# Attention and a two-layer MLP on one core: the exponentials instead of V as the stationary operand of the second attention product, normalised on the way out of PSUM, with the loads on SyncE's queue

## The chip, the cores and the metric

The kernel runs on one core of a Trainium2 chip. The metric is device time in microseconds (us). Before the change three runs gave a median of 557.68 us (556.79 to 560.31).

## The reference

```python
# q, k, v: [8, 12, 448, 64] float32; w_in: [768, 2048], w_out: [2048, 768]
scores = scale * np.matmul(q, k.transpose(0, 1, 3, 2))
scores = scores - np.max(scores, axis=-1, keepdims=True)
attn = np.exp(scores)
attn = attn / (np.sum(attn, axis=-1, keepdims=True) + 1e-09)
attn_out = np.matmul(attn, v)
x = attn_out.transpose(0, 2, 1, 3).reshape(B * S, H * D)     # 3584 x 768
h = x @ w_in
g = np.maximum(0.01 * h, h)
out = g @ w_out                                              # 3584 x 768
```

## The kernel before

Two heads of one batch element make a *unit*; there are 48 units, six to each of the eight batch elements. A sequence of 448 positions is cut into four chunks of 112 (`SC`, `NSC`), taken with a stride of four so that each partition reads contiguous memory. The work of a unit is:

- `load` fetches q, k and v in float32, three DMAs of 224 KB issued by GpSimd. `cast` turns them into bf16 on GpSimd, v into one of four tiles `v_sb` whose other 64 columns hold ones.
- `transposes` turns q and k on TensorE (eight transposes into the PSUM tile `tr`), and VectorE copies the result out as `qkT`.
- `scores` makes the transposed scores, keys on partitions, for one chunk of keys and both heads; `expo` takes the exponential on ScalarE into `e`. Four such chunks make a unit. The PSUM tiles `sc` have two buffers.
- `pv(u, j)` multiplies for head j: V with its ones is stationary (112 x 128), the exponentials stream past with 448 columns, four matmuls accumulate over the key chunks. The result has head dimension on partitions; 64 of its rows all hold the sum of the exponentials. VectorE copies it out as `t`, and a DMA on SyncE's queue brings one row of sums into a small tile.
- `recips` inverts the sums on VectorE, writes them to DRAM by one DMA, and reads them back by two, spread over 64 partitions each (`rb`). `muls` multiplies `t` by `rb` on VectorE into `xT`, the MLP's input, in two pieces for each head since the MLP's token blocks are cut at multiples of 128.
- `mlp(i)` takes 384 or 512 tokens: 96 matmuls with `w_in` (line 233), leaky ReLU on ScalarE, then 32 matmuls for each 128 tokens with `w_out` (line 245), copied out by VectorE and stored by SyncE's queue.

Every engine runs its instructions in the order in which they are written here. `slots(u)` gives eight steps of work of unit u, in which `pv` belongs to unit u-1 and `recips` and `muls` to unit u-2. The loop at the end writes the steps of six units and hands out the matmuls of one `mlp` evenly between them. The first `mlp` begins after the first step of unit 8, so units 0 to 7 run without MLP work beside them; the last `mlp` stands alone at the end. The weights are loaded by GpSimd's queue, two pieces at a time in the first four units, and each is cast from float32 by its DMA.

Of the kernel before, what the change touches and what calls it, by code (L numbers as in the profile page):

```python
# [9 lines left out]
F32 = mybir.dt.float32  # L10
BF16 = mybir.dt.bfloat16
AX = mybir.ActivationFunctionType
PSUM = bass.MemoryType.PSUM
DRAM = bass.MemoryType.DRAM


@with_exitstack
def kernel(
# [27 lines left out]
    const_pool = ctx.enter_context(tc.tile_pool(name="const", bufs=1))  # L46
    w_pool = ctx.enter_context(tc.tile_pool(name="weights", bufs=1))
    ld_pool = ctx.enter_context(tc.tile_pool(name="ld", bufs=6))
    cast_pool = ctx.enter_context(tc.tile_pool(name="cast", bufs=3))
    v_pool = ctx.enter_context(tc.tile_pool(name="vones", bufs=1))  # L50
    qk_pool = ctx.enter_context(tc.tile_pool(name="qk", bufs=3))
    exp_pool = ctx.enter_context(tc.tile_pool(name="exp", bufs=3))
    t_pool = ctx.enter_context(tc.tile_pool(name="pvt", bufs=3))
    r_pool = ctx.enter_context(tc.tile_pool(name="rec", bufs=3))
    xT_pool = ctx.enter_context(tc.tile_pool(name="xT", bufs=3))
    h_pool = ctx.enter_context(tc.tile_pool(name="h", bufs=2))
    o_pool = ctx.enter_context(tc.tile_pool(name="o", bufs=3))
    d_pool = ctx.enter_context(tc.tile_pool(name="drec", bufs=4, space=DRAM))

    ps_s = ctx.enter_context(tc.tile_pool(name="ps_s", bufs=2, space=PSUM))  # L60
    ps_tr = ctx.enter_context(tc.tile_pool(name="ps_tr", bufs=1, space=PSUM))
    ps_pv = ctx.enter_context(tc.tile_pool(name="ps_pv", bufs=1, space=PSUM))
    ps_mm = ctx.enter_context(tc.tile_pool(name="ps_mm", bufs=2, space=PSUM))

    ident = const_pool.tile([P, P], BF16)
    make_identity(nc, ident)

    NV = 4  # L70
    v_sb = [v_pool.tile([SC, 2, NSC, 2 * D], BF16, name=f"v{i}") for i in range(NV)]
    for t in v_sb:
        nc.vector.memset(t[:, 0, :, D:], 1.0)
        nc.vector.memset(t[:, 1, :, :D], 1.0)

    w_in_sb = w_pool.tile([P, KD, DF], BF16)
    w_out_sb = w_pool.tile([P, MD, DM], BF16)
# [4 lines left out]
    q_sb = {}  # L82
    k_sb = {}

    def load(u):
        if u >= NU:
            return
        b, hp = divmod(u, HP)  # L90
        raw[u] = []
        for a, name in ((q, "fq"), (k, "fk"), (v, "fv")):
            t = ld_pool.tile([SC, 2, NSC, D], F32, name=name)
            nc.gpsimd.dma_start(  # L94
                out=t.rearrange("p h so d -> p h (so d)"),
                in_=a[b, 2 * hp:2 * hp + 2].rearrange("h (p so) d -> p h (so d)", so=NSC),
            )
            raw[u].append(t)

    def cast(u):  # L100
# [5 lines left out]
        nc.gpsimd.tensor_copy(q_sb[u].rearrange("p so h d -> p h so d"), fq)  # L106
        nc.gpsimd.tensor_copy(k_sb[u].rearrange("p so h d -> p h so d"), fk)  # L107
        for j in range(2):
            nc.gpsimd.tensor_copy(v_sb[u % NV][:, j, :, j * D:(j + 1) * D], fv[:, j])  # L109

    load(0)
    cast(0)
    load(1)
    load(2)
    load(3)
    cast(1)
    for i in range(4, 6):
        load(i)
# [6 lines left out]
    def load_w(n):  # L125
        for _ in range(n):
            if w_steps:
                o, i = w_steps.pop(0)
                nc.gpsimd.dma_start(out=o, in_=i)


    qk_t = {}
    e_t = {}
    pv_s = {}
    bc_t = {}
    xT = [None] * (B + 1)

    def get_xT(i):
        if xT[i] is None:
            xT[i] = xT_pool.tile([P, KD, 4 * P], BF16, name="xT")  # L140
        return xT[i]

    def transposes(u):
        b, hp = divmod(u, HP)
        tr = ps_tr.tile([P, 2, S], BF16, name="tr")
        for i, src in enumerate((q_sb[u], k_sb[u])):
            for so in range(NSC):
                nc.tensor.transpose(  # L148
                    tr[:, i, ts(so, SC)], src[:, so], ident[:SC, :SC]
                )  # L150
        qk_t[u] = qk_pool.tile([P, 2, S], BF16, name="qkT")
        nc.vector.tensor_copy(qk_t[u], tr)  # L152

    sc_t = {}
# [10 lines left out]
            )  # L165

    def expo(u, c):
        if u not in e_t:
            e_t[u] = exp_pool.tile([SC, 2, NSC, S], BF16, name="e")
        nc.scalar.activation(e_t[u][:, :, c, :], sc_t.pop((u, c))[:, :, :S], AX.Exp, scale=scale)  # L170

    def pv(u, j):
        b, hp = divmod(u, HP)
        ps = ps_pv.tile([P, S], F32, name="pv")
        for c in range(NSC):
            nc.tensor.matmul(  # L176
                ps, v_sb[u % NV][:, j, c, :], e_t[u][:, j, c, :],
                start=(c == 0), stop=(c == NSC - 1),
            )
        t = t_pool.tile([P, S], F32, name=f"t{j}")  # L180
        nc.vector.tensor_copy(t, ps)  # L181
        pv_s[u, j] = t
        if j == 0:
            bc_t[u] = r_pool.tile([SC, 2, NSC], F32, name="sums")
        row = t[D:D + 1, :] if j == 0 else t[0:1, :]
        nc.sync.dma_start(out=bc_t[u][:, j, :], in_=row)

    def recips(u):
        rec = r_pool.tile([SC, 2, NSC], F32, name="rec")
        nc.vector.reciprocal(rec, bc_t[u])  # L190
        d = d_pool.tile([2, S], F32, name="d")
        nc.sync.dma_start(out=d.rearrange("j (p c) -> p j c", c=NSC), in_=rec)
        rb = r_pool.tile([P, S], F32, name="rb")
        for j in range(2):
            nc.sync.dma_start(out=rb[ts(j, D), :], in_=d[j:j + 1, :].to_broadcast([D, S]))  # L195
        bc_t[u] = rb

    def muls(u):
        b, hp = divmod(u, HP)
        lo, hi = b * S, (b + 1) * S  # L200
        for j in range(2):
            pl = slice(j * D, (j + 1) * D)
            for i in (b, b + 1):
                a, z = max(lo, cuts[i]), min(hi, cuts[i + 1] if i < B else hi)
                if a >= z:
                    continue
                x = get_xT(i)
                nc.vector.tensor_mul(  # L208
                    x[pl, hp, a - cuts[i]:z - cuts[i]],
                    pv_s[u, j][pl, a - lo:z - lo],  # L210
                    bc_t[u][pl, a - lo:z - lo],
                )
        del pv_s[u, 0], pv_s[u, 1], bc_t[u], e_t[u], qk_t[u]


    def store(o, t0):
# [38 lines left out]
    def slots(u):  # L255

        on = u < NU

        def s0():
            if on:  # L260
                scores(u, 0)
                scores(u, 1)
                expo(u, 0)
            load(u + 6)
            if u < 6:
                load_w(2)

        def s1():
            if on:
                expo(u, 1)  # L270
            if u >= 2:
                recips(u - 2)

        def s2():
            if 1 <= u <= NU:
                pv(u - 1, 0)

        def s3():
            cast(u + 2)

        def s4():
            if on:
                scores(u, 2)
                scores(u, 3)
                expo(u, 2)

        def s5():
            if on:
                expo(u, 3)

        def s6():
            if 1 <= u <= NU:
                pv(u - 1, 1)

        def s7():
            if u + 1 < NU:
                transposes(u + 1)
            if u >= 2:
                muls(u - 2)

        return [s0, s1, s2, s3, s4, s5, s6, s7]

# [48 lines left out]
```

## Time and profile before

| | before |
|---|---|
| median of 3 runs | 557.68 us |
| the profiled execution | 556.75 us |
| its span, first to last instruction | 555.0 us |
| TensorE busy in matmuls | 478.5 us (86%) |
| VectorE, ScalarE, GpSimd busy | 215.2, 231.3, 202.1 us |
| mean granted TensorE clock | 0.937 of 2.4 GHz |

The profiled execution took 1.75 us more than its span, and the median of the runs is 0.93 us above it. TensorE's busy time counts the modelled end of each matmul, so matmuls overlap in it; where its pace matters, the distance from one start to the next is the better reading. The busy share is also a mean over a first stage, in which TensorE often stands still, and a long middle in which it seldom does.

### The profile page before, as it was taken

To read this page: it belongs to the slowest core of one execution; us is meant where nothing else is said; L and a number is where in the kernel's file an instruction comes from. 1 tells how busy PE (TensorE), PEld (TensorE's weight loads), DVE (VectorE), ACT (ScalarE), POOL (GpSimd) and SP (SyncE) were. 2 spreads that over 40 slices of the span, in tenths; PEclk is the share of its full clock that TensorE was granted. 3 is DMA by queue.
4 is the path that set the end of the run, shared out by engine and by line. 5 is a ranking of instruction groups with operands and counts; after the bars stand their busy time and mean duration, and the time that the engine had idled before them with its cause. 6 is when DMAs were issued, how large, how long until landed. Compare 5 with 4: busy or idle time off the path is not lost.

```text
span 555.0 us, 7636 instructions
## 1 busy us (share of the span) xinstructions
PE 478.5 (86%) x2816; PEld 237.6 (43%) x2816; DVE 215.2 (39%) x400; ACT 231.3 (42%) x321; POOL 202.1 (36%) x350
## 2 busy tenths in 40 slices
PE   2744447999899999999599999999699999996996
PEld 1211113455444554555244554555244555552453
DVE  2221335444433564444234545464253553341011
ACT  3332223563346334654165335644365246601400
POOL 8963724454532433643225335455141210000000
PEclk9998555999989999999799999999899999997999
DMA  5999944344533354535433436354341222122013
GB/s 147 249 230 242 242 109 103 98 118 120 156 96 83 89 155 123 135 90 154 113 82 94 122 102 172 97 145 115 95 118 30 79 62 50 31 63 60 1 28 87
DMA packets 52774, 62.21 MB, mean 112 GB/s; under 512 B 28672, under 2 KB 39936, under 8 KB 52736
## 3 DMA queue, kind: packets, MB, share of 16 engines
q0 software_dynamic: 16768, 39.33, 27.8%
q1 hardware_dynamic: 35968, 22.38, 16.6%
q8 instruction: 22, 0.36, 0.3%
q14 instruction: 16, 0.13, 0.1%
HBM read 56.62 MB, written 11.18 MB: 122 GB/s over the span
## 4 chain that ended last, share of the span: by engine, by line
PE 65%; DMA 22%; DVE 7%; SPq 2%; issue 2%; POOL 2%; DVEq 0%; POOLq 0%
PE mm L233 25%; PE mm L245 19%; PE pv L176 11%; DMA d<-rec 8%; DMA sums<-t 7%; DMA rb<-d 7%; PE sc L160 6%; DVE xT L208 3%; PE tr L148 3%; DVE qkT L152 2%; SPq L195 1%; DVE o L250 1%; DMA fv<-in_v_dram 1%; SPq L224 1%; POOL fq L94 0%
## 5 line engine op out<-in xcount | busy, mean ns | idle before, releaser
L170 ACT ACTIVATE e<-sc 112x896 bf16<-112x896 f32 x192 | 168.5, 915 | 188.8 <-PE sc L160 188.6
L233 PE MATMUL mm<-xT,w_in_sb 128*128 128x384 bf16 (+1 forms) x768 | 173.0, 364 | 20.9 <-DVE xT L208 19.4
L245 PE MATMUL mm<-w_out_sb,h 128*128 128x384 bf16 x896 | 162.1, 326 | 0.8 <-DVE o L250 0.6
L176 PE MATMUL pv<-e,v 112*128 112x448 bf16 x384 | 100.9, 390 | 29.9 <-DVE t L181 29.9
L109 POOL CAST v<-fv 112x256 bf16<-112x256 f32 x96 | 38.3, 404 | 230.9 <-PE pv L176 230.6
L181 DVE COPY t<-pv 128x448 f32<-128x448 f32 x96 | 59.6, 620 | 149.0 <-PE pv L176 148.7
L233 PEld LDWEIGHTS <-w_in_sb 128*128 128x128 bf16 x768 | 72.0, 100 | 102.7 <-issue 47.7
L238 ACT ACTIVATE h<-mm 128x384 bf16<-128x384 f32 (+1 forms) x128 | 69.9, 546 | 109.2 <-PE mm L233 109.1
L208 DVE TENSOR_TENSOR xT<-t,rb 64x384 bf16<-64x384 f32 (+2 forms) x144 | 87.1, 630 | 68.2 <-DMA rb<-d 67.0
L245 PEld LDWEIGHTS <-h 128*128 128x128 bf16 x896 | 83.6, 98 | 67.0 <-issue 13.7
L176 PEld LDWEIGHTS <-v 112*128 112x128 bf16 x384 | 38.9, 103 | 74.7 <-issue 47.8
L160 PE MATMUL sc<-qkT 64*112 64x448 bf16 x384 | 63.4, 411 | 8.6 <-DVE qkT L152 6.4
L250 DVE COPY o<-mm 128x384 f32<-128x384 f32 x56 | 31.1, 555 | 63.6 <-PE mm L245 63.1
L152 DVE COPY qkT<-tr 128x896 bf16<-128x896 bf16 x48 | 30.0, 624 | 33.5 <-PE tr L148 32.8
L160 PEld LDWEIGHTS <-qkT 64*112 64x112 bf16 x384 | 18.7, 135 | 45.6 <-DVE qkT L152 24.8
L94 POOL DMA_DIRECT2D fv<-in_v_dram x48 | 31.9, 664 | 11.9 <-DMA w_in_sb<-in_moe_w_in_dram 6.5
L106 POOL CAST q<-fq 112x512 bf16<-112x512 f32 x48 | 34.0, 708 | 4.2 <-PE tr L148 1.5
L94 POOL DMA_DIRECT2D fk<-in_k_dram x48 | 31.9, 665 | 7.2 <-DMA w_out_sb<-in_moe_w_out_dram 4.6
L94 POOL DMA_DIRECT2D fq<-in_q_dram x48 | 32.1, 668 | 4.6 <-issue 0.2
L107 POOL CAST k<-fk 112x512 bf16<-112x512 f32 x48 | 31.8, 662 | 0.1
L148 PE MATMUL tr<-ident,q 112*128 112x112 bf16 x192 | 19.3, 228 | 11.2 <-POOL q L106 11.2
L148 PEld LDWEIGHTS <-q 112*128 112x128 bf16 x192 | 15.4, 106 | 21.1 <-POOL q L106 12.4
(14 smaller groups left out, 52.8 us busy)
## 6 DMA issues: line engine op xcount, KB each, us to landing
fq<-in_q_dram POOLq DMA_DIRECT2D x48, 224.0 KB, 3.4
fk<-in_k_dram POOLq DMA_DIRECT2D x48, 224.0 KB, 3.9
fv<-in_v_dram POOLq DMA_DIRECT2D x48, 224.0 KB, 4.2
rb<-d SPq DMA_DIRECT2D x96, 112.0 KB, 3.0
w_in_sb<-in_moe_w_in_dram POOLq DMA_DIRECT2D x4, 768.0 KB, 12.7
w_out_sb<-in_moe_w_out_dram POOLq DMA_DIRECT2D x4, 768.0 KB, 17.7
out_dram<-o SPq DMA_DIRECT2D x8, 336.0 KB, 3.3
out_dram<-o SPq DMA_DIRECT2D x8, 288.0 KB, 2.7
```

The costliest lines, as they stand in the source:

```text
L94: nc.gpsimd.dma_start(out=t.rearrange("p h so d -> p h (so d)"), in_=a[b, 2 * hp:2 * hp + 2].rearrange("h (p so) d -> p h (so d)", so=NSC),)
L109: nc.gpsimd.tensor_copy(v_sb[u % NV][:, j, :, j * D:(j + 1) * D], fv[:, j])
L148: nc.tensor.transpose(tr[:, i, ts(so, SC)], src[:, so], ident[:SC, :SC])
L152: nc.vector.tensor_copy(qk_t[u], tr)
L160: nc.tensor.matmul(ps[:, j, :S], qk_t[u][j * D:(j + 1) * D, 1, ts(c, SC)], qk_t[u][j * D:(j + 1) * D, 0, :], start=True, stop=True,)
L170: nc.scalar.activation(e_t[u][:, :, c, :], sc_t.pop((u, c))[:, :, :S], AX.Exp, scale=scale)
L176: nc.tensor.matmul(ps, v_sb[u % NV][:, j, c, :], e_t[u][:, j, c, :], start=(c == 0), stop=(c == NSC - 1),)
L181: nc.vector.tensor_copy(t, ps)
L208: nc.vector.tensor_mul(x[pl, hp, a - cuts[i]:z - cuts[i]], pv_s[u, j][pl, a - lo:z - lo], bc_t[u][pl, a - lo:z - lo],)
L233: nc.tensor.matmul(ps[:, :n], w_in_sb[:, kk, ts(m, P)], get_xT(i)[:, kk, :n], start=(kk == 0), stop=(kk == KD - 1),)
L238: nc.scalar.activation(h[:, m, :n], ps[:, :n], AX.Prelu, alpha=0.01)
L245: nc.tensor.matmul(ps[:, :NW], h[:, m, ts(c, P)], w_out_sb[:, m, ts(w, NW)], start=(m == 0), stop=(m == MD - 1),)
```

## The change

`pv` swaps its operands. For each chunk of 112 queries the exponentials (112 keys x 128 columns, of which 112 are the queries and 16 run on into the next bytes) are stationary, and V with a single column of ones (65 columns) streams past, accumulated over four chunks of keys: 16 matmuls a head instead of four. The result has queries on partitions and its sum in column 64, so VectorE takes the reciprocal of four values for each partition from PSUM and multiplies straight out of PSUM into a bf16 tile `x`. `x_transposes` then turns `x` by four TensorE transposes for each unit, and VectorE copies them into `xT`. The copies `t`, the DMAs of sums, `d` and `rb`, and the products from `t` and `rb` are gone. The loads are issued by SyncE's queue (one of the first by ScalarE's), all casts of v take one instruction, casts run three units ahead instead of two, buffers of `v_sb` and the casts become five and four, the weights are issued one piece at a time (one ahead of the loop, one each in units 0 to 2 and 5 to 8), and each `mlp` begins six steps earlier, right behind the step that holds the last `x_transposes` it needs.

```diff
-    v_sb = [v_pool.tile([SC, 2, NSC, 2 * D], BF16, name=f"v{i}") for i in range(NV)]
+    v_sb = [v_pool.tile([SC, 2, NSC, D + 1], BF16, name=f"v{i}") for i in range(NV)]
+    EL = 2 * NSC * S
+    e_sb = [exp_pool.tile([SC, EL + P - SC], BF16, name=f"e{i}") for i in range(NE)]
...
-    def load(u):
+    def load(u, queues=(nc.sync,) * 3):
...
-            nc.gpsimd.dma_start(
+            eng.dma_start(
...
-        for j in range(2):
-            nc.gpsimd.tensor_copy(v_sb[u % NV][:, j, :, j * D:(j + 1) * D], fv[:, j])
+        by[2](v_sb[u % NV][:, :, :, :D], fv)
...
+    load(0, (nc.sync, nc.scalar, nc.sync))
+    for i in range(1, 6):
+        load(i)
...
+    cast(0, (nc.vector.tensor_copy, nc.scalar.copy, nc.gpsimd.tensor_copy))
+    load_w()
+    cast(1)
+    cast(2)
...
     def pv(u, j):
-        ps = ps_pv.tile([P, S], F32, name="pv")
-        for c in range(NSC):
-            nc.tensor.matmul(
-                ps, v_sb[u % NV][:, j, c, :], e_t[u][:, j, c, :],
-                start=(c == 0), stop=(c == NSC - 1),
-            )
-        t = t_pool.tile([P, S], F32, name=f"t{j}")
-        nc.vector.tensor_copy(t, ps)
...
+        e, vt = e_sb[u % NE], v_sb[u % NV]
+        ps = ps_pv.tile([P, NSC, D + 1], F32, name="pv")
+        for qc in range(NSC):
+            for c in range(NSC):
+                at = (j * NSC + c) * S + qc * SC
+                nc.tensor.matmul(
+                    ps[:, qc, :], e[:, at:at + P], vt[:, j, c, :],
+                    start=(c == 0), stop=(c == NSC - 1),
+                )
         if j == 0:
-            bc_t[u] = r_pool.tile([SC, 2, NSC], F32, name="sums")
-        row = t[D:D + 1, :] if j == 0 else t[0:1, :]
-        nc.sync.dma_start(out=bc_t[u][:, j, :], in_=row)
+            x_t[u] = x_pool.tile([SC, NSC, 2, D], BF16, name="x")
+        rec = r_pool.tile([SC, NSC, 1], F32, name="rec")
+        nc.vector.reciprocal(rec, ps[:SC, :, D:])
+        nc.vector.tensor_mul(
+            x_t[u][:, :, j, :], ps[:SC, :, :D], rec.to_broadcast([SC, NSC, D])
+        )
...
-    def recips(u):
...
-    def muls(u):
+    def x_transposes(u):
         b, hp = divmod(u, HP)
         lo, hi = b * S, (b + 1) * S
+        tr = ps_tr.tile([P, 2, S], BF16, name="tr")
+        for so in range(NSC):
+            nc.tensor.transpose(tr[:, 0, ts(so, SC)], x_t[u][:, so], ident[:SC, :SC])
+        for i in (b, b + 1):
+            a, z = max(lo, cuts[i]), min(hi, cuts[i + 1] if i < B else hi)
+            if a < z:
+                nc.vector.tensor_copy(
+                    get_xT(i)[:, hp, a - cuts[i]:z - cuts[i]], tr[:, 0, a - lo:z - lo]
+                )
...
         def s0():
-            load(u + 6)
-            if u < 6:
-                load_w(2)
         def s1():
-            if u >= 2:
-                recips(u - 2)
+            if 2 <= u <= NU + 1:
+                x_transposes(u - 2)
         def s3():
-            cast(u + 2)
+            load(u + 6)
         def s5():
+            cast(u + 3)
+            if u <= 2 or 5 <= u <= 8:
+                load_w()
         def s7():
-            if u >= 2:
-                muls(u - 2)
...
+    begin = [8 * (HP * (i + 1) + 1) + 2 for i in range(B)]
     transposes(0)
-    for i in range(B + 1):
-        first = 0 if i == 0 else HP * i + 2
-        last = HP * (i + 1) + 2 if i < B else first
-        work = [s for u in range(first, min(last, NU + 2)) for s in slots(u)]
-        atoms = mlp(i - 1) if i > 0 else iter(())
+    for s in steps[:begin[0]]:
+        s()
+    for i in range(B):
+        work = steps[begin[i]:begin[i + 1]] if i + 1 < B else []
+        atoms = mlp(i)
```

## Rows read from the trace of the kernel before

**Rows 1.** Windows by stage: length, busy us (count) by engine, clock, DMA share, GB/s

```profile
0.00:95.60 95.60, 47.10 (x196) 18.22 (x196) 26.04 (x57) 28.96 (x34) 58.50 (x105) 0.77 0.86 189
95.60:500.60 405.00, 386.53 (x2399) 196.98 (x2398) 182.92 (x332) 192.75 (x272) 143.58 (x246) 0.98 0.39 103
500.60:506.40 5.80, 1.23 (x7) 0.47 (x6) 1.28 (x3) 0.00 (x0) 0.00 (x0) 0.94 0.18 40
506.40:555.00 48.60, 43.68 (x219) 21.96 (x218) 4.98 (x9) 9.56 (x16) 0.00 (x0) 0.92 0.15 41
```

**Rows 2.** TensorE's waits, first 95 us: waiter, releaser, total us, times, longest

```profile
PE pv L176 <- DVE t L181: 29.9, 5, 11.2
PE tr L148 <- POOL q L106: 11.2, 3, 5.6
```

**Rows 3.** Timeline of VectorE and TensorE around one stall of the first stage

```profile
55.25 0.69 DVE L208 TENSOR_TENSOR xT<-t,rb 64x384 bf16<-64x384 f32 x2 [10.73 <-DMA rb<-d]
...
59.35 0.53 PE L176 MATMUL pv<-e,v 112*128 112x448 bf16 x1 [11.25 <-DVE t L181]
```

**Rows 4.** TensorE's waits from 95 us to the end

```profile
PE mm L233 <- DVE xT L208: 19.4, 7, 5.8
```

**Rows 5.** TensorE's timeline of the end: start us, length us, instructions

```profile
500.57 1.24 PE L233 MATMUL mm<-xT,w_in_sb 128*128 128x512 bf16 x5
506.38 22.90 PE L233 MATMUL mm<-xT,w_in_sb 128*128 128x512 bf16 x91 [4.57 <-DVE xT L208]
529.12 20.96 PE L245 MATMUL mm<-w_out_sb,h 128*128 128x384 bf16 x128
```

**Rows 6.** TensorE's timeline of one unit in the middle stage

```profile
463.02 0.59 PE L160 MATMUL sc<-qkT 64*112 64x448 bf16 x4
463.54 1.48 PE L233 MATMUL mm<-xT,w_in_sb 128*128 128x384 bf16 x8
464.85 0.92 PE L176 MATMUL pv<-e,v 112*128 112x448 bf16 x4
465.61 1.47 PE L233 MATMUL mm<-xT,w_in_sb 128*128 128x384 bf16 x8
...
470.24 0.36 PE L148 MATMUL tr<-ident,q 112*128 112x112 bf16 x4
470.44 0.36 PE L148 MATMUL tr<-ident,k 112*128 112x112 bf16 x4
...
471.52 0.59 PE L160 MATMUL sc<-qkT 64*112 64x448 bf16 x4
```

**Rows 7.** TensorE's timeline in the first stage: end of unit 0, one unstalled unit

```profile
10.06 0.62 PE L160 MATMUL sc<-qkT 64*112 64x448 bf16 x2 [0.19 <-ACT e L170]
...
25.01 0.99 PE L160 MATMUL sc<-qkT 64*112 64x448 bf16 x4 [0.72 <-DVE qkT L152]
25.93 1.68 PE L176 MATMUL pv<-e,v 112*128 112x448 bf16 x4
27.54 0.99 PE L160 MATMUL sc<-qkT 64*112 64x448 bf16 x4
...
29.93 0.58 PE L148 MATMUL tr<-ident,q 112*128 112x112 bf16 x4
30.31 0.58 PE L148 MATMUL tr<-ident,k 112*128 112x112 bf16 x4
31.61 0.62 PE L160 MATMUL sc<-qkT 64*112 64x448 bf16 x2 [0.72 <-DVE qkT L152]
```

**Rows 8.** Groups by line and shape: busy us, mean ns, idle before

```profile
L170 ACT ACTIVATE e<-sc 112x896 bf16<-112x896 f32 x192 | 168.5, 915 | 188.8 <-PE sc L160 188.6
L208 DVE TENSOR_TENSOR xT<-t,rb 64x384 bf16<-64x384 f32 x48 | 37.0, 770 | 34.9 <-DMA rb<-d 34.2
L190 DVE RECIPROCAL rec<-sums 112x8 f32<-112x8 f32 x48 | 9.7, 203 | 20.3 <-DMA sums<-t 19.2
```

**Rows 9.** Window of the heaviest loading, same columns as the first group

```profile
20.00:48.00 28.00, 17.09 (x71) 6.18 (x68) 6.65 (x14) 9.40 (x12) 19.84 (x34) 1.00 1.20 234
```

More of the change, by code (lines that the diff above doesn't have):

```diff
@@ L13 @@
 PSUM = bass.MemoryType.PSUM
-DRAM = bass.MemoryType.DRAM
 @with_exitstack
@@ L48 @@
     ld_pool = ctx.enter_context(tc.tile_pool(name="ld", bufs=6))
-    cast_pool = ctx.enter_context(tc.tile_pool(name="cast", bufs=3))
+    cast_pool = ctx.enter_context(tc.tile_pool(name="cast", bufs=4))
     v_pool = ctx.enter_context(tc.tile_pool(name="vones", bufs=1))
     qk_pool = ctx.enter_context(tc.tile_pool(name="qk", bufs=3))
-    exp_pool = ctx.enter_context(tc.tile_pool(name="exp", bufs=3))
-    t_pool = ctx.enter_context(tc.tile_pool(name="pvt", bufs=3))
-    r_pool = ctx.enter_context(tc.tile_pool(name="rec", bufs=3))
+    exp_pool = ctx.enter_context(tc.tile_pool(name="exp", bufs=1))
+    r_pool = ctx.enter_context(tc.tile_pool(name="rec", bufs=4))
+    x_pool = ctx.enter_context(tc.tile_pool(name="x", bufs=3))
     xT_pool = ctx.enter_context(tc.tile_pool(name="xT", bufs=3))
@@ L57 @@
     o_pool = ctx.enter_context(tc.tile_pool(name="o", bufs=3))
-    d_pool = ctx.enter_context(tc.tile_pool(name="drec", bufs=4, space=DRAM))
     ps_s = ctx.enter_context(tc.tile_pool(name="ps_s", bufs=2, space=PSUM))
@@ L63 @@
     ps_mm = ctx.enter_context(tc.tile_pool(name="ps_mm", bufs=2, space=PSUM))
-    ident = const_pool.tile([P, P], BF16)
-    make_identity(nc, ident)
-    NV = 4
-    v_sb = [v_pool.tile([SC, 2, NSC, 2 * D], BF16, name=f"v{i}") for i in range(NV)]
-    for t in v_sb:
-        nc.vector.memset(t[:, 0, :, D:], 1.0)
-        nc.vector.memset(t[:, 1, :, :D], 1.0)
+    NV = 5
+    v_sb = [v_pool.tile([SC, 2, NSC, D + 1], BF16, name=f"v{i}") for i in range(NV)]
+    NE = 3
+    EL = 2 * NSC * S
+    e_sb = [exp_pool.tile([SC, EL + P - SC], BF16, name=f"e{i}") for i in range(NE)]
     w_in_sb = w_pool.tile([P, KD, DF], BF16)
@@ L91, in load @@
         raw[u] = []
-        for a, name in ((q, "fq"), (k, "fk"), (v, "fv")):
+        for a, name, eng in zip((q, k, v), ("fq", "fk", "fv"), queues):
             t = ld_pool.tile([SC, 2, NSC, D], F32, name=name)
-            nc.gpsimd.dma_start(
+            eng.dma_start(
                 out=t.rearrange("p h so d -> p h (so d)"),
@@ L98, in load, with cast @@
             raw[u].append(t)
-    def cast(u):
+    def cast(u, by=(nc.gpsimd.tensor_copy,) * 3):
         if u >= NU:
@@ L105, in cast @@
         k_sb[u] = cast_pool.tile([SC, NSC, 2, D], BF16, name="k")
-        nc.gpsimd.tensor_copy(q_sb[u].rearrange("p so h d -> p h so d"), fq)
-        nc.gpsimd.tensor_copy(k_sb[u].rearrange("p so h d -> p h so d"), fk)
-        for j in range(2):
-            nc.gpsimd.tensor_copy(v_sb[u % NV][:, j, :, j * D:(j + 1) * D], fv[:, j])
[L111 to L118, printed above, removed]
+        by[0](q_sb[u].rearrange("p so h d -> p h so d"), fq)
+        by[1](k_sb[u].rearrange("p so h d -> p h so d"), fk)
+        by[2](v_sb[u % NV][:, :, :, :D], fv)
     w_steps = []
@@ L123, with load_w @@
         w_steps.append((w_out_sb[:, ts(i, MD // 4), :], w_out_v[:, ts(i, MD // 4), :]))
-    def load_w(n):
+    def load_w(n=1):
         for _ in range(n):
@@ L129, in load_w @@
                 nc.gpsimd.dma_start(out=o, in_=i)
+    load(0, (nc.sync, nc.scalar, nc.sync))
+    for i in range(1, 6):
+        load(i)
+    ident = const_pool.tile([P, P], BF16)
+    make_identity(nc, ident)
+    for t in v_sb:
+        nc.gpsimd.memset(t[:, :, :, D:], 1.0)
+    for t in e_sb:
+        nc.gpsimd.memset(t[:, EL:], 0.0)
+    cast(0, (nc.vector.tensor_copy, nc.scalar.copy, nc.gpsimd.tensor_copy))
+    load_w()
+    cast(1)
+    cast(2)
     qk_t = {}
-    e_t = {}
-    pv_s = {}
-    bc_t = {}
+    x_t = {}
     xT = [None] * (B + 1)
@@ L143, in transposes @@
     def transposes(u):
-        b, hp = divmod(u, HP)
         tr = ps_tr.tile([P, 2, S], BF16, name="tr")
@@ L167, in expo @@
     def expo(u, c):
-        if u not in e_t:
-            e_t[u] = exp_pool.tile([SC, 2, NSC, S], BF16, name="e")
-        nc.scalar.activation(e_t[u][:, :, c, :], sc_t.pop((u, c))[:, :, :S], AX.Exp, scale=scale)
+        e = e_sb[u % NE][:, :EL].rearrange("p (j c s) -> p j c s", j=2, c=NSC)
+        nc.scalar.activation(e[:, :, c, :], sc_t.pop((u, c))[:, :, :S], AX.Exp, scale=scale)
     def pv(u, j):
-        b, hp = divmod(u, HP)
-        ps = ps_pv.tile([P, S], F32, name="pv")
-        for c in range(NSC):
-            nc.tensor.matmul(
-                ps, v_sb[u % NV][:, j, c, :], e_t[u][:, j, c, :],
-                start=(c == 0), stop=(c == NSC - 1),
-            )
@@ L180, in pv @@
-        t = t_pool.tile([P, S], F32, name=f"t{j}")
-        nc.vector.tensor_copy(t, ps)
-        pv_s[u, j] = t
-        if j == 0:
-            bc_t[u] = r_pool.tile([SC, 2, NSC], F32, name="sums")
-        row = t[D:D + 1, :] if j == 0 else t[0:1, :]
-        nc.sync.dma_start(out=bc_t[u][:, j, :], in_=row)
-    def recips(u):
[L189 to L196, printed above, removed]
@@ L199, in muls @@
+        rec = r_pool.tile([SC, NSC, 1], F32, name="rec")
[4 more added lines that the diff above has]
+    def x_transposes(u):
         b, hp = divmod(u, HP)
         lo, hi = b * S, (b + 1) * S
[L201 to L211, printed above, removed]
+        tr = ps_tr.tile([P, 2, S], BF16, name="tr")
[6 more added lines that the diff above has]
+                    get_xT(i)[:, hp, a - cuts[i]:z - cuts[i]], tr[:, 0, a - lo:z - lo]
@@ L212, in muls @@
                 )
-        del pv_s[u, 0], pv_s[u, 1], bc_t[u], e_t[u], qk_t[u]
+        del x_t[u], qk_t[u]
     def store(o, t0):
@@ L297, in s7 @@
                 transposes(u + 1)
-            if u >= 2:
-                muls(u - 2)
         return [s0, s1, s2, s3, s4, s5, s6, s7]
+    steps = [s for u in range(NU + 2) for s in slots(u)]
+    begin = [8 * (HP * (i + 1) + 1) + 2 for i in range(B)]
+    assert begin[B - 1] == 8 * (NU + 1) + 2
     transposes(0)
-    for i in range(B + 1):
-        first = 0 if i == 0 else HP * i + 2
-        last = HP * (i + 1) + 2 if i < B else first
-        work = [s for u in range(first, min(last, NU + 2)) for s in slots(u)]
-        atoms = mlp(i - 1) if i > 0 else iter(())
-        total = 0 if i == 0 else MD * KD * (cuts[i] - cuts[i - 1]) + (cuts[i] - cuts[i - 1]) // P * MD * DM
+    for s in steps[:begin[0]]:
+        s()
+    for i in range(B):
+        work = steps[begin[i]:begin[i + 1]] if i + 1 < B else []
+        n = cuts[i + 1] - cuts[i]
+        total = MD * KD * n + n // P * MD * DM
         used = 0
-        for n, s in enumerate(work):
+        atoms = mlp(i)
+        for j, s in enumerate(work):
             s()
-            while used < total * (n + 1) // len(work):
+            while used < total * (j + 1) // len(work):
                 step = next(atoms, None)
```

## The prediction

> **What bounds the kernel now.** I first cut the span into stages by windows [rows 1]. For 95.6 us, until the first MLP matmul, TensorE is busy 47 us. From 95.6 to 500.6 us it is busy 386.5 of 405 us. Then come 5.8 us with almost nothing, and 48.6 us of the last MLP alone. The page's shares average over these.
>
> Next I read the waits of the first stage [rows 2]: `pv` waits 29.9 us for VectorE's copies `t`, the transposes 11.2 us for GpSimd's casts. One stall shows the mechanism [rows 3]: VectorE stands 10.73 us in the product that needs `rb`, the copy of a later unit's `pv` is queued behind it in order, and TensorE, whose only `pv` buffer is not emptied, stands 11.25 us. So the round trip sums, reciprocal, DRAM, `rb` sets the first stage. In the middle the same trip shows only where an `mlp` starts: 19.4 us of waits for `xT` [rows 4], of which 4.57 us lie in the gap before the last `mlp` [rows 5].
>
> Otherwise TensorE sets the pace there. Its prices, from starts to starts: an MLP matmul of 384 columns 1.31 us / 8 = 0.164 [rows 6], in the tail 20.96 / 128 = 0.164; one of 512 columns, 22.74 us for 91, less half of the 6 us at half clock (the granted 0.92 of 48.6 us is 8 us at 1.2 GHz, of which some 6 are here), gives 0.216 [rows 1, 5]. All MLP work is 384 x 0.216 + 384 x 0.164 + 896 x 0.164 = 293 us. A unit costs scores 2 x 0.52, `pv` 2 x 0.76, transposes 2 x 0.20; its period of 8.50 us less 32 x 0.164 and these leaves 0.29 of small gaps [rows 6].
>
> Check on before, from 95.6 us: 41 `pv`, 39.5 scores, 39 transposes and 39.5 gaps are left, 62 + 41 + 16 + 12 = 131; with 293, 19 of waits, 8 + 4 lost to half clock [rows 1], and 5 from the last matmul to the end [rows 5], this is 460; the trace has 459.4. So the sum may be used for the new kernel.
>
> **The change, part by part.**
>
> *The swapped product.* Per unit, 8 matmuls of 448 columns (1.52 us) become 32 pairs of a 128-column weight load and a 65-column matmul. The nearest row is the transpose of q, with the same load (112 partitions by 128 columns) and 112 columns moving: four take 0.20 us, 50 ns a pair [rows 6]. If the columns set that, 65 give 28 ns; if the load does, 50 stays. Per unit 0.90 to 1.60 us; I take the middle, 39 ns and 1.25 us, since no row divides the two. The four new transposes cost 4 x 50 ns = 0.20. So a unit in the middle stage changes by -0.07 us (-0.4 to +0.3): nearly nothing.
>
> Here a page speaks against the change. The Trainium skill ("TensorE: Matmul & The Clock Gate", Back-to-back issue gap) puts a stream of load and matmul pairs at about 81 ns each at 128 columns; this trace's transposes run at 50. By the page, an estimate of 32 x 81 ns = 2.6 us a unit, the result would be some 55 us later.
>
> *The normalisation.* Gone: two copies, five DMAs and four products a unit. Added on VectorE: two reciprocals of about 0.20 us (row of eight values), two products of 256 values at 770 ns / 384 each, 0.51 us [rows 8], and copies of half a `tr`. VectorE is busy 183 of 405 us in the middle [rows 1] and does less after; this costs nothing there. The stalls of 30 us go, and so does the wait before the MLPs. New waits: `x_transposes` for the product, with scores, transposes and MLP matmuls queued behind it on TensorE. In the middle its cover is the MLP work of three steps (some 2.5 us) against 0.7 us on VectorE. It also shares the one `tr` buffer with q and k; two steps lie between. An `mlp` now starts behind half a `pv` (0.6 us) and needs the last unit's rows only at its sixth matmul (0.8 more), against half a microsecond of copying. Without cover this costs about 0.6 us at each of eight MLPs; I allow 6 us for all remaining waits and clock.
>
> *The loads.* GpSimd loses three issues a unit and keeps casts; it was busy 58.5 of 95.6 us in the first stage [rows 1] and kept the transposes waiting [rows 2]. SyncE's queue loses five DMAs a unit and gains three loads. A load now stands behind a store that waits for its `o`, but it is issued six units ahead, 50 us of cover by the period of rows 6; I cost it at nothing. Casts three units ahead and the split weight pieces cost GpSimd, not the path. The DMA limit: by the start of the first `mlp` units 0 to 7 and one weight piece must be in, 8 x 0.69 + 0.8 = 6.3 MB, 27 us at the 234 GB/s of the heaviest window [rows 9]. It is not the bound while the first stage lasts over 35 us.
>
> *The first stage* is where the time goes. Without a stall a unit took 31.61 - 25.01 = 6.60 us [rows 7]. Its matmuls run at half clock: `pv` takes 1.61 a head where the middle has 0.76 (the clock column's 1.00 in rows 9 is contradicted by this pace). Take out 2 x 1.61. Put in 32 pairs: transposes take 0.38 / 4 = 95 ns here, so 55 to 95 ns, 1.8 to 3.0 us. Add four transposes, 0.38, and 0.3 (0.1 to 0.4) because `qkT` now queues behind reciprocal and product (0.71 us) instead of one copy. That gives 5.9 to 7.1 us. At full clock: 1.04 + 0.40 + 0.20 + 0.9 to 1.6 plus some 1.3 of waits for `qkT` is 3.8 to 4.5; ScalarE's four exponentials, 4 x 0.915 = 3.66 [rows 8], allow 4.3. Unit 0's scores end at about 11 us [rows 7]; six units follow, then 2.2 to 2.8 us to the first MLP matmul (one half-unit of scores, four transposes, one `pv`). At half clock the first `mlp` starts at 48 to 57 us, at full clock at 38.6. I take 49: mostly half clock, as the rows show, and some full.
>
> *The sum.* From then on: 293 MLP, 41.5 `pv` x 1.25 = 52, 40.5 scores 42, 40 transposes 16, 42 new transposes 8, 40.5 gaps 12, allowance 6, end 5. That is 49 + 434 = 483 us of span. With the 1.75 us outside it, 485 for an execution like the profiled one; the median of before stands 0.9 above its profile, so 485 to 486. Against 557.7, some 46 us come from the first stage and some 25 from waits and clock.
>
> **The rivals.**
>
> *The first stage runs warm.* TensorE has no long stop there any more, so the clock may rise early. The first `mlp` then starts at 38.6, and the time is about 475; with 28 ns pairs 41.5 x 32 x 11 ns = 15 less, 460. Against it: the unstalled stretch of rows 7 was at half clock.
>
> *The weight load isn't hidden.* A 65-column matmul could be too short to cover the next load, and a pair be load and matmul in a row: 50 + 28 = 78 ns. That is 39 ns x 32 x 41.5 = 52 us more, plus some in the first stage: about 540, still faster. Against: transposes overlap the two.
>
> *TensorE isn't fed fast enough: slower.* Its instructions in such a unit rise from 112 to 168 (64 of MLP, 16 of scores, 24 of transposes, 64 of `pv`, loads counted). Before, one left every 8.50 / 112 = 76 ns. If instructions could arrive only at that pace, a unit would take 12.8 us, and the time would pass 650. It decides from 8.50 + 1.8 = 10.3 us a unit, 61 ns an instruction: there the whole gain of 72 us is spent, and slower supply than that loses. For it: no row shows a long run much faster. Against: 16 instructions of transposes leave in 0.40 us, 25 ns each [rows 6], though these may have been waiting in a queue. The Trainium skill (the same page, Wait — 56ns, not 53.3ns?) names about 62 ns for each matmul where the sequencer decodes in software; no run here shows which way this chip decodes, and by the matmuls alone, an estimate of 84 x 62 ns = 5.2 us a unit, it would not bind.
>
> *The change doesn't do what it says.* If loads on SyncE's queue came late, TensorE would wait at the transposes as before, at most the 11 us of rows 2: about 496.
>
> **How the numbers follow.** The forecast, with late loads inside it: 0.75. Warm first stage: 0.11. Load not hidden: 0.07. Starved TensorE: 0.07, of which 0.05 ends slower and 0.02 near no change. The unknowns' ends are 38.6 + 293 + 115 + 3 + 5 = 455 and 57 + 293 + 145 + 12 + 5 = 512 of span; the range of 8 in 10 is 460 to 512, leaving out the unhidden load, the starved engine and the best end. A run of this kernel tells about 1% from no change. Faster by over 1%: 0.93; within 1%: 0.02; slower: 0.05.
>
> **What would show it.** First MLP matmul near 49 us, and which clock is granted before it; no long waits for VectorE before it; a middle unit of 384 tokens at 8.1 to 8.8 us; starts of `pv` pairs 28 to 50 ns apart; no gap before the last `mlp`. I am wrong if pairs of `pv` stand 80 ns apart or more, if TensorE idles with nothing to wait for, or if the granted clock falls in the middle stage.

## The result, and the profile after

The changed kernel takes 460.29 us (median of 4, 459.46 to 461.3) against 557.23 us (550.83 to 560.31): a ratio of 0.829, 95% interval 0.822 to 0.837. The forecast was 485, its range 460 to 512; the time lies 0.3 us inside the range's lower edge, and close to the 460 that the rival "the first stage runs warm" gave with its shortest pairs. The profiled execution took 459.46 us, its span 457.7 us.

The same stages by windows (length, busy us by engine with counts, clock, DMA share, GB/s), to be read against [rows 1]:

```profile
0.00:41.55 41.55, 27.32 (x357) 17.88 (x358) 14.80 (x45) 26.23 (x31) 20.26 (x45) 1.00 1.10 249
41.55:457.70 416.15, 409.10 (x3792) 236.64 (x3805) 122.96 (x326) 204.51 (x292) 71.75 (x120) 1.00 0.37 98
```

The first MLP matmul comes at 41.55 us, before at 95.6: 54 us are gained there. From it to the end are 416 us, before 459: another 43 us gained. The page's slices show TensorE at 9 from the fifth slice to the last but one. The granted clock reads full speed from the start to 456 us, where before it had fallen four times after the first stage (0.98 and 0.92 in [rows 1]). Up to 20 us the pace of the matmuls contradicts the column, as it did in [rows 9]; where this text says that the clock rose, it goes by the pace.

All of TensorE's waits:

```profile
PE sc L157 <- DVE qkT L149: 6.5, 8, 0.9
PE tr L145 <- DVE q L101: 5.0, 1, 5.0
PE sc L157 <- ACT e L166: 2.5, 6, 0.6
```

The 29.9 us for `t` and 11.2 us for casts [rows 2] and the 19.4 us for `xT` [rows 4] are gone. The 5.0 us are the wait for the first load and its cast; the rest is a unit's own chain in the first stage.

TensorE's timeline of one unit in the middle (start us, length us), against [rows 6]:

```profile
271.41 0.58 PE L157 MATMUL sc<-qkT 64*112 64x448 bf16 x4
271.93 0.82 PE L219 MATMUL mm<-xT,w_in_sb 128*128 128x384 bf16 x4
272.59 0.36 PE L192 MATMUL tr<-ident,x 112*128 112x112 bf16 x4
272.79 0.81 PE L219 MATMUL mm<-xT,w_in_sb 128*128 128x384 bf16 x4
273.44 0.68 PE L175 MATMUL pv<-v,e 112*128 112x65 bf16 x16
273.95 1.47 PE L219 MATMUL mm<-xT,w_in_sb 128*128 128x384 bf16 x8
...
279.62 0.59 PE L157 MATMUL sc<-qkT 64*112 64x448 bf16 x4
```

Sixteen pairs take 273.95 - 273.44 = 0.51 us, 32 ns each, where four matmuls of 448 columns took 0.76. The unit is 8.21 us instead of 8.50. The first stage and the end:

```profile
12.34 1.06 PE L175 MATMUL pv<-v,e 112*128 112x65 bf16 x16
13.33 1.14 PE L157 MATMUL sc<-qkT 64*112 64x448 bf16 x4
...
20.14 0.69 PE L175 MATMUL pv<-v,e 112*128 112x65 bf16 x16
20.67 0.36 PE L145 MATMUL tr<-ident,q 112*128 112x112 bf16 x4
...
26.65 0.58 PE L157 MATMUL sc<-qkT 64*112 64x448 bf16 x4 [0.87 <-DVE qkT L149]
27.17 0.37 PE L192 MATMUL tr<-ident,x 112*128 112x112 bf16 x4
...
31.20 0.59 PE L157 MATMUL sc<-qkT 64*112 64x448 bf16 x4 [0.87 <-DVE qkT L149]
...
410.67 0.81 PE L231 MATMUL mm<-w_out_sb,h 128*128 128x384 bf16 x4
411.54 20.67 PE L219 MATMUL mm<-xT,w_in_sb 128*128 128x512 bf16 x94
432.05 20.96 PE L231 MATMUL mm<-w_out_sb,h 128*128 128x384 bf16 x128
```

At 12 us the pairs still take 0.99 us / 16 = 62 ns, half clock; at 20.14 us they take 0.53 / 16 = 33 ns, full clock. After this rise a unit takes 31.20 - 26.65 = 4.55 us, before 6.60 without a stall and at half clock [rows 7]. The last MLP follows without a gap, where [rows 5] had 4.57 us.

### The profile page after: what moved, and what is told of

The parts are those of the page before. It is cut to its first block, busy times and chain, and to the rows that moved or that the text cites. A ratio compares the mean times of both kernels' runs of the same rounds, so it can differ in the third digit from the quotient of the medians.

```text
span 457.7 us, 9871 instructions
## 1 busy us (share of the span) xinstructions
PE 436.4 (95%) x4143; PEld 254.5 (56%) x4160; DVE 137.8 (30%) x369; ACT 230.7 (50%) x322; POOL 92.0 (20%) x164
## 4 chain that ended last, share of the span: by engine, by line
PE 90%; DVE 5%; issue 1%; ACT 1%; DMA 1%; ACTq 0%
PE mm L231 31%; PE mm L219 31%; PE sc L157 11%; PE pv L175 11%; PE tr L145 4%; DVE qkT L149 4%; PE tr L192 2%; ACT e L166 1%; DMA fq<-in_q_dram 1%; DVE x L183 0%; DVE rec L182 0%; DVE o L236 0%; DVE q L101 0%; ACTq L166 0%
## 5 line engine op out<-in xcount | busy, mean ns | idle before, releaser
L219 PE MATMUL mm<-xT,w_in_sb 128*128 128x384 bf16 (+1 forms) x751 | 164.5, 352 | 0.9
L219 PEld LDWEIGHTS <-w_in_sb 128*128 128x128 bf16 x768 | 66.6, 97 | 62.6 <-issue 14.2
L103 POOL CAST v<-fv 112x512 bf16<-112x512 f32 x48 | 29.6, 616 | 243.3 <-PE pv L175 228.3
L175 PEld LDWEIGHTS <-e 112*128 112x128 bf16 x1536 | 62.1, 99 | 15.1 <-issue 1.5
L175 PE MATMUL pv<-v,e 112*128 112x65 bf16 x1536 | 66.1, 195 | 0.0
L182 DVE RECIPROCAL rec<-pv 112x4 f32<-112x4 f32 x96 | 17.5, 182 | 115.2 <-PE pv L175 115.0
L157 PEld LDWEIGHTS <-qkT 64*112 64x112 bf16 x384 | 18.8, 128 | 43.9 <-DVE qkT L149 24.6
L196 DVE COPY xT<-tr 128x384 bf16<-128x384 bf16 (+1 forms) x72 | 20.3, 309 | 72.2 <-PE tr L192 72.2
L183 DVE TENSOR_TENSOR x<-pv,rec 112x256 bf16<-112x256 f32 x96 | 40.7, 424 | 3.3
L149 DVE COPY qkT<-tr 128x896 bf16<-128x896 bf16 x48 | 29.9, 622 | 23.7 <-PE tr L145 23.6
L192 PEld LDWEIGHTS <-x 112*128 112x128 bf16 x192 | 13.8, 98 | 8.7 <-issue 2.4
L145 PE MATMUL tr<-ident,k 112*128 112x112 bf16 x192 | 17.9, 218 | 0.0
```

Source lines behind the costliest of these rows:

```text
L103: by[2](v_sb[u % NV][:, :, :, :D], fv)
L145: nc.tensor.transpose(tr[:, i, ts(so, SC)], src[:, so], ident[:SC, :SC])
L157: nc.tensor.matmul(ps[:, j, :S], qk_t[u][j * D:(j + 1) * D, 1, ts(c, SC)], qk_t[u][j * D:(j + 1) * D, 0, :], start=True, stop=True,)
L175: nc.tensor.matmul(ps[:, qc, :], e[:, at:at + P], vt[:, j, c, :], start=(c == 0), stop=(c == NSC - 1),)
L183: nc.vector.tensor_mul(x_t[u][:, :, j, :], ps[:SC, :, :D], rec.to_broadcast([SC, NSC, D]))
L219: nc.tensor.matmul(ps[:, :n], w_in_sb[:, kk, ts(m, P)], get_xT(i)[:, kk, :n], start=(kk == 0), stop=(kk == KD - 1),)
```

## The experiments

Two questions were open: what had held the first stage, and what sets the pair of load and matmul. In one further place the runs look for what is late next.

**The loads in the loop back on GpSimd's queue** (changed kernel):

```diff
-            load(u + 6)
+            load(u + 6, (nc.gpsimd,) * 3)
```

> The changed kernel with the loads of units 6 to 47 issued by GpSimd's queue again (the first six units' stay on SyncE's and ScalarE's). Theory (the loads' queue is worth little, the normalisation's round trip was the bound): 459 to 464 us; in the first stage GpSimd would have 1.8 us of casts, 2.0 us of issues and 0.9 us for a piece of weights in a unit of 4.55 us, so it is just not the bound. Rival (GpSimd issuing loads in line with casts was a large part of the first stage): the casts come late, the first MLP matmul moves from 41.6 us to 50 us or later, 470 us or more.

462.64 us (462.14 to 463.57), ratio to before 0.833 (0.827 to 0.839); the first MLP matmul at 41.7 us. The queue of these loads is worth little, as the theory said. The interval overlaps that of the changed kernel, so the 2.3 us more are hardly clear of the noise; the trace has one new wait, 2.0 us for `w_out`. The first six units' loads, the weights' order and the casts' longer lead stay here as in the changed kernel, so the run tells of the loop's loads alone.

**The loads alone on SyncE's queue** (kernel before):

```diff
-            nc.gpsimd.dma_start(
+            nc.sync.dma_start(
                 out=t.rearrange("p h so d -> p h (so d)"),
```

> The kernel before with its loads on SyncE's queue and nothing else changed. Theory: the round trip through DRAM still sets the first stage, so at most the 11 us of waits for casts go: 545 to 560 us, the first MLP matmul still past 80 us. Rival (the loads on GpSimd were the cause): the first MLP matmul at 50 to 60 us, about 515 us.

One execution, the profiled one, took 1619 us beside three of 546.7 to 551.8 (median 546.8) and is left out with its trace. Ratio 0.987 (0.978 to 0.996), a gain of about 7 us (2 to 12), as the theory said. The kernel ran once more for a trace:

> The kernel before with its loads on SyncE's queue, once more, for a trace without a disturbance. Theory: about 549 us, pv waiting for VectorE's copies 20 us or more in the first stage, and the waits for casts mostly gone. Rival (loads behind the round trip's DMAs in SyncE's order come late): waits for casts of 10 us or more remain.

551.76 us; the first MLP matmul at 92.5 us. Two rows of TensorE's waits in the first 95 us, and the timeline of SyncE's queue, VectorE and TensorE:

```profile
PE pv L176 <- DVE t L181: 35.4, 6, 17.6
PE tr L148 <- POOL q L106: 4.4, 1, 4.4
```

```profile
21.98 2.39 SPq L186 DMA_DIRECT2D sums<-t  x2
25.76 0.33 SPq L94 DMA_DIRECT2D fq<-in_q_dram  x1
...
36.70 0.20 DVE L190 RECIPROCAL rec<-sums 112x8 f32<-112x8 f32 x1 [19.47 <-DMA sums<-t]
...
37.44 1.65 PE L176 MATMUL pv<-e,v 112*128 112x448 bf16 x4 [17.55 <-DVE t L181]
```

The waits for casts mostly go, but the waits for VectorE grow from 29.9 to 35.4 us. The last of two DMAs of 1.8 KB is issued by 24.4 us, and its data are used at 36.7, 12 us later; on this queue it stands among the loads. So the loads' move alone makes the round trip worse. The queue need not be the whole reason. GpSimd, freed of the loads, issues all eight pieces of the weights between 10 and 22 us, before between 21 and 47; the DMA share up to 20 us is 0.99 instead of 0.68, and in the first 48 us a load takes some 8 us to land instead of 5. No run divides the shared queue from the weights that come earlier.

**More slack for the round trip** (kernel before, product, round trip and loads untouched):

```diff
-            if u >= 2:
-                recips(u - 2)
+            if 3 <= u <= NU + 2:
+                recips(u - 3)
...
-            if u >= 2:
-                muls(u - 2)
+            if u >= 4:
+                muls(u - 4)
```

Each MLP begins two units later with it, and there are more buffers (`t` 4, `drec` 6).

> The kernel before with its product, its round trip and its loads as they are, but the reciprocals one unit later and the products with rb two units later, and each MLP two units later with them. Theory (the first stage stood on VectorE waiting in order for the round trip): the 30 us of pv waits shrink to under 5, two more units pass before the first MLP matmul, and that comes at 60 to 75 us; the waits for xT at the MLPs go: 490 to 515 us. If the clock rises early here as well, the lower end. Rival (the swapped product itself, or the lighter VectorE, made the gain): the first stage stays over 85 us and the time over 535 us.

519.9 us (518.96 to 521.14), ratio 0.936 (0.930 to 0.942): 36 us less than before without the swapped product. But the size missed: the first MLP matmul came at 91.6 us, not 60 to 75, and the rival had said over 85. So only 4 of the 36 us came before it, though two more units stand there now; the rest came behind it, where two units fewer are left and the waits for `xT` fell from 19.4 us [rows 4] to 3.0. TensorE's waits in the first 91 us, and GpSimd's longest:

```profile
PE tr L148 <- POOL q L106: 19.1, 6, 5.4
PE sc L160 <- DVE qkT L152: 8.0, 11, 0.9
PE pv L176 <- DVE t L181: 7.0, 3, 4.0
```

```profile
POOL fv L94 <- DMA w_in_sb<-in_moe_w_in_dram: 7.8, 2, 4.3
```

The waits for the round trip fell to 7.0 us, and the casts took their place with 19.1: GpSimd casts in order behind its own load issues, and these wait for the weights' DMAs.

**Slack and the loads on SyncE's queue together:**

> The kernel before with both: more slack for the round trip, as in the run with the slack alone (519.9 us), and the loads on SyncE's queue, as in the run with the loads alone (549.3 us). Theory (round trip and casts behind GpSimd's loads stand one behind the other: when the first no longer stops TensorE, the second does): the 19 us of waits for casts that the slack left go, the first MLP matmul moves from 91.6 us to 65 to 75 us, 490 to 505 us, much more than the 7 us that the loads alone gave. Rival (the two parts are independent, or SyncE's queue makes loads wait behind the round trip's DMAs): 511 to 520 us.

522.71 us (521.87 to 523.4), ratio 0.940 (0.933 to 0.946); the first MLP matmul at 95.4 us. My theory that the two stand one behind the other fell, and the time lies above the rival's 520 too. TensorE's waits in the first 95 us:

```profile
PE pv L176 <- DVE t L181: 26.4, 5, 10.6
...
PE tr L148 <- POOL q L106: 4.6, 1, 4.6
```

The casts come in time, and the `pv` waits are back at 26.4 us, although there is more slack: the small DMAs are late again. In the first 48 us a DMA of sums takes 12.4 us to land (median of four), in the run with the slack alone 6.2 (median of six), and the weights are again all issued by 22 us. That gave the theory that the round trip is long because it shares queue and DMA engines with loads and weights. The chain that ended last, in the kernel before (start us, length us), has hops (one step of the round trip, from issue to landing) of 5 to 8 us in the first stage; below it stands the DMA row of the page (share in tenths, slices of 13.9 us):

```profile
21.45 5.79 DMA sums<-t
...
27.57 5.96 DMA d<-rec
...
40.95 7.98 DMA d<-rec
```

```profile
DMA  5999944344533354535433436354341222122013
```

**The kernel before without the loads of units 6 to 47** (their casts read the tiles of units 0 to 5 again, so the output is not the reference's; the weights are still loaded):

```diff
+        if u >= 6:
+            raw[u] = kept[u % 6]
+            return
         b, hp = divmod(u, HP)
-        raw[u] = []
+        raw[u] = kept[u] = []
```

> The kernel before with the loads of units 6 to 47 left out (their casts read the tiles of units 0 to 5 again); the weights are still loaded. Theory (the round trip's small DMAs are slow because loads and weights fill the DMA engines in the first stage; they take 5 to 8 us there and 2.5 to 3 us later): once the weights are in, at about 45 us, each hop takes some 3 us, the pv waits after that go, and the first MLP matmul comes at 70 to 80 us instead of 95.6: 525 to 540 us. Rival (the round trip of four DMAs is too long for its one unit of slack even on quiet DMA engines): pv waits of several us each remain after 45 us, the first MLP matmul after 85 us, 543 us or more.

525.14 us (524.34 to 526.31), ratio 0.949 (0.942 to 0.956); the first MLP matmul at 80.1 us. The same chain, and the DMA row (slices of 13.1 us):

```profile
28.11 6.21 DMA d<-rec
...
42.69 6.70 DMA d<-rec
...
56.74 2.31 DMA d<-rec
59.07 2.95 DMA rb<-d
```

```profile
DMA  5999211012311221112201321022201231121012
```

From 13 to 52 us the DMA row is at 9 and a hop takes 6 to 7 us; from 57 us on, with the weights in, a hop takes 1.5 to 3 us and `pv` waits at most 0.57 us. The same round trip of three hops and five DMAs, with the same slack, holds `pv` up only while the DMA engines are full. This theory holds. It is not the whole first stage: the `pv` waits up to 57.3 us still sum to 18 us and those for casts to 9.8, and at the starts of the MLPs 7.6 us of waits for `xT` remain. The time is at the lower end of the theory's range, the first MLP matmul just past its 80 us.

**Each MLP six steps later** (changed kernel):

```diff
-    begin = [8 * (HP * (i + 1) + 1) + 2 for i in range(B)]
+    begin = [8 * (HP * (i + 1) + 2) for i in range(B)]
...
```

> The changed kernel with each MLP beginning six steps later, as the kernel before had it. Theory: three quarters of a unit more without MLP work beside it, at 4.55 us where its own TensorE work is some 2.6: 461 to 463 us. Rival (starting the MLP right behind the last transposes keeps a wait that a later start would hide, at seven MLPs): 455 to 459 us.

462.42 us (461.49 to 462.67), ratio 0.832 (0.827 to 0.837): 2 us more, as expected, though the interval overlaps that of the changed kernel. The first MLP matmul came at 47.0 us; the clock rose only at 26.7 us, so not all of that move is the six steps.

**The stationary exponentials cut to the 112 columns in use** (changed kernel):

```diff
-                    ps[:, qc, :], e[:, at:at + P], vt[:, j, c, :],
+                    ps[:SC, qc, :], e[:, at:at + SC], vt[:, j, c, :],
```

> The changed kernel with the stationary exponentials cut to the 112 columns that are used (the result's 112 partitions). Theory A (a pair's 32 ns are its 65 columns, and the load is hidden whatever its width): pairs stay at 31 to 33 ns, 458 to 462 us. Theory B (a load of 128 columns takes a faster path, which 112 don't get): a pair takes about 112 columns at full clock, 47 ns, and 41.5 x 32 x 15 ns = 20 us are added, 478 to 490 us.

499.61 us (498.72 to 500.12), ratio 0.906 (0.901 to 0.911): 39 us more than the changed kernel for loading 16 columns fewer. Two groups of weight loads between 100 and 400 us (busy us, mean ns, idle), and the timeline:

```profile
L175 PEld LDWEIGHTS <-e 112*112 112x112 bf16 x983 | 60.6, 132 | 7.9
L231 PEld LDWEIGHTS <-h 128*128 128x128 bf16 x605 | 53.4, 99 | 37.8 <-issue 10.8
```

```profile
40.17 1.66 PE L175 MATMUL pv<-v,e 112*112 112x65 bf16 x16
41.76 0.99 PE L157 MATMUL sc<-qkT 64*112 64x448 bf16 x4
...
275.34 0.97 PE L175 MATMUL pv<-v,e 112*112 112x65 bf16 x16
276.14 1.79 PE L231 MATMUL mm<-w_out_sb,h 128*128 128x384 bf16 x10
```

A pair takes 0.80 / 16 = 50 ns instead of 32: theory B, and 41.5 x 32 x 18 ns = 24 us. Another 14 us, which puts the time above theory B's 490, is what I had left out: in the first stage a pair takes 1.59 / 16 = 99 ns, the clock rose only at 57 us, and the first MLP matmul came at 55.6 us. The Trainium skill ("TensorE: Matmul & The Clock Gate", Weight-path perf modes) says that the fast weight load is on when there are 128 weight columns and the type is not FP32; this trace agrees, 132 ns for a load of 112 columns against 99 for one of 128. The kernel before had such rows too, the scores' loads of 112 columns with a mean of 135 ns over the whole span and those of V of 128 columns with 103:

```profile
L160 PEld LDWEIGHTS <-qkT 64*112 64x112 bf16 x384 | 18.7, 135 | 45.6 <-DVE qkT L152 24.8 <-issue 20.8
L176 PEld LDWEIGHTS <-v 112*128 112x128 bf16 x384 | 38.9, 103 | 74.7 <-issue 47.8
```

**Half of V** (changed kernel; the first 32 columns of V are left out, and their place in `x` is filled with the others' product):

```diff
-                    ps[:, qc, :], e[:, at:at + P], vt[:, j, c, :],
+                    ps[:, qc, D // 2:], e[:, at:at + P], vt[:, j, c, D // 2:],
...
```

> The changed kernel with 33 columns moving instead of 65: the first half of V's columns is left out, and its place in x is filled with the second half's product. Theory A (the columns set the pair): pairs at 16 to 18 ns, 41.5 x 32 x 15 ns = 20 us less, 438 to 446 us. Theory B (the load, or the rate at which instructions arrive, is a floor near 30 ns): pairs stay at 28 to 32 ns, 454 to 461 us.

454.2 us (453.76 to 454.67), ratio 0.824 (0.819 to 0.828): the time is at the lower end of theory B, the pair between the two theories.

```profile
271.23 0.56 PE L175 MATMUL pv<-v,e 112*128 112x33 bf16 x16
271.64 1.46 PE L221 MATMUL mm<-xT,w_in_sb 128*128 128x384 bf16 x8
```

0.41 / 16 = 25 to 26 ns a pair: half the columns save 6 ns, where the columns alone would have saved 16, so something else sets a floor near 25 ns. The 65 columns, at 32, are still above it. The runs don't say whether the load or the arrival of instructions sets the floor. The Trainium skill (the same page, Wait — 56ns, not 53.3ns?) names about 25 ns as the least distance from one matmul to the next however few the columns; these pairs, each with its own load, agree. The saving is 41.5 x 32 x 6 to 7 ns = 8 to 9 us; 2.4 of it were lost since the first MLP matmul came at 43.9 us, with the clock rising only at 46 us.

**The transposes of q and k four steps earlier** (changed kernel), to shorten the 4.55 us of a unit in the first stage:

```diff
         def s3():
+            if u + 1 < NU:
+                transposes(u + 1)
             load(u + 6)
...
         def s7():
-            if u + 1 < NU:
-                transposes(u + 1)
+            pass
```

> The changed kernel with the transposes of q and k of the next unit four steps earlier (in the fourth step of a unit instead of the eighth). Theory (the first stage's unit of 4.55 us is ScalarE's 3.66 us of exponentials and the wait for qkT ahead of the scores, since ScalarE stands 1.2 us for the scores): the wait goes, a unit takes 3.7 to 4.0 us, the first MLP matmul comes at 36 to 39 us, 454 to 458 us. Rival (the first stage is bound by the arrival of loads and weights, whose DMA share is 1.1): no change, 459 to 461 us, the first MLP matmul at 41 to 42 us.

458.53 us (456.26 to 459.26), ratio 0.831 (0.826 to 0.835). Units take 4.1 us and the first MLP matmul comes at 38.0 us, 3.5 earlier, within the theory's 36 to 39, but only 1.8 us are left at the end, and the time lies just above its 458. Two new waits of TensorE:

```profile
PE mm L231 <- DMA w_out_sb<-in_moe_w_out_dram: 2.2, 1, 2.2
PE tr L145 <- POOL k L102: 2.1, 2, 1.4
```

The granted clock also fell to half for 3.4 us (69.4 to 72.8 us) behind the first of them. The gain is given back where data arrive late. Two variants of this run shift the DMAs, the first the weights alone:

```diff
-            if u <= 2 or 5 <= u <= 8:
+            if 2 <= u <= 8:
```

> The run with earlier transposes (458.5 us), and the second to fourth piece of w_in issued in units 2 to 4 instead of 0 to 2. Theory (its first stage of 4.1 us a unit is now limited by loads that share the DMA engines with weights): the waits for casts, 2 us, go; the MLP's wait for w_out, 2 us, stays or grows: 456 to 459 us. Rival (the arrival of data has no part): 458 to 459 us with the same waits.

460.3 us (457.64 to 462.54): the waits for casts went, the wait for `w_out` grew to 5.1 us. Nothing gained: the waits went as the theory said, but the time lies above its 459. The second issues the weights in units 1 to 7 and loads fewer units ahead:

```diff
-            load(u + 6)
+            if u < 3:
+                load(u + 6)
+            elif u >= 5:
+                load(u + 4)
...
-            if u <= 2 or 5 <= u <= 8:
+            if 1 <= u <= 7:
```

> The run with earlier transposes, the weights' pieces issued in units 1 to 7, no loads issued in units 3 and 4, and loads four units ahead from unit 5 on. Theory (all weights and too many loads want the DMA engines before 69 us, where the last piece of w_out was waited for): both the waits for casts and the wait for w_out go, 452 to 456 us. Rival (loads four units ahead come too late): new waits for casts in the middle, 458 us or more.

457.34 us (456.84 to 458.5), ratio to before 0.822 (0.817 to 0.827), first MLP matmul at 37.7 us: between the theory's 456 and the rival's 458. The casts' wait went (0.2 us left), the `w_out` wait stayed (3.0 us), so the theory is half right. Its six runs lie below all four of the changed kernel; the intervals of the two ratios overlap, and they ran in different groups, so 3 us is the best estimate of the gain, and no more.

## Why the prediction was right, and where it was off

**The bound.** Right in the main: the longest waits of the first stage were for the round trip, they are gone, and the first MLP matmul moved by 54 us, against 46 forecast. What share of the 54 us the trip has by itself is not shown. The casts' longer lead and the weights' new order changed with it, and I had costed them at nothing on the path; in the kernel before, more slack for the trip alone brought 19.1 us of waits for casts, with GpSimd waiting for the weights. No run changes that lead and that order by themselves. The loads' queue gave about 7 us by itself in the kernel before and at most about 2 in the new one. What the prediction lacked is why the trip was long. I put its cost down to VectorE's order and took its DMAs as given; the runs that leave out or shift loads show that a hop lasts 5 to 8 us while loads and weights fill the DMA engines, and 1.5 to 3 us otherwise.

**The first stage's length** was mis-sized: 49 us taken, 41.55 measured. The term was the clock, "mostly half clock, as the rows show, and some full": the pace was full from 20 us on. A unit at half clock also cost a little less than the 5.9 to 7.1 us of the sum, 22.75 - 17.00 = 5.75 us in the run with later MLPs. My all-warm figure was 38.6 with 4.3 us a unit; the warm unit is 4.55, and units 0, 1 and most of 2 ran cold. So the rival of the warm first stage, with a chance of 0.11, came nearer than the forecast, and the time is inside the range by 0.3 us only: the range was right by its width, not by its middle.

**The pair** was mis-sized: 39 ns taken from bounds of 28 to 50, 32 measured, 41.5 x 32 x 7 ns = 9 us. The row of 112 moving columns was set by its columns, not by its load, and the run with 112 stationary columns shows that this rests on the full 128: with the narrower load the pair is at my upper bound. The 81 ns that the Trainium skill names for a pair at 128 columns ("TensorE: Matmul & The Clock Gate", Back-to-back issue gap) found no support here: 50 ns at 112 columns and 32 at 65.

**The allowance** of 6 us for waits and clock was not used: after the first stage TensorE has no wait worth a row, and the granted clock stays up until the last two microseconds.

Together this is 7.5 + 9 + 6 of the 25.5 us by which 485 exceeds the profiled 459.5; the other 3 us lie in the rest of the prices. All of them erred to the same side.

**The rivals.** The unhidden load was not met as built (32 ns, not 78). The starved TensorE was not met: 168 instructions leave in 8.21 us, 49 ns each on average and 16 ns within a `pv`, under the 61 ns at which the gain would have been gone. Late loads were not met in the changed kernel; waits for casts and weights appear as soon as the first stage is shortened.

**The middle unit**, 8.21 us, lies in the stated 8.1 to 8.8; the last MLP follows without a gap, as forecast.

## What to carry to other kernels

A small DMA in a dependent chain costs what the queue and the DMA engines carry at that moment, here 1.5 to 3 us quiet and 5 to 8 us under loads; price it from the stretch where it runs, and before moving other DMAs to its queue ask what it will queue behind and what the queue that is freed will issue earlier. When short products are made of pairs of load and matmul, look at the load's shape first: here 16 unused columns were worth 39 us. And when one wait is removed, name the next one in the same stage: casts, small DMAs and weights each took its place in one of the runs.

## What was not expected of the hardware

By its pace TensorE went from half to full clock at 20.2 us in the changed kernel, 14.8 us in the run with the loop's loads on GpSimd and 26.7 us in the one with later MLPs, though its work up to the earlier of two such moments is the same, and at 46 and 57 us in the runs with half of V and with narrow loads, there soon after the first MLP matmuls (43.9 and 55.6 us). The column of the granted clock reads 1.00 all that time. After the first load TensorE had stood for 0.9 us at most at a time in each of them. In the run with the loop's loads on GpSimd the granted clock fell again before the MLP, behind no longer waits than that (window, length, busy us by engine with counts, clock, DMA share, GB/s):

```profile
35.30:38.70 3.40, 3.40 (x37) 2.14 (x36) 1.06 (x4) 2.37 (x3) 2.54 (x5) 0.50 1.18 218
```

What decides these moments stays open; their effect on the time was at most a few us where the pair was 32 ns. The execution of 1619 us is another open case: TensorE alone was slow in it, with an MLP matmul of 384 columns every 0.64 us (569.6 us for 896) instead of 0.164, while the granted clock reads 1.00 and ScalarE's exponentials last 914 ns as ever.
